# A three-part kernel on one core: 32-bit low words in the weight narrowing, attention buffers laid out by when the last batch frees them, and a new written order

## The chip, the cores and the metric

One core of a Trainium2 chip runs the whole program. The metric is the device time of one execution in microseconds (us). TensorE (PE) does the matmuls, VectorE (DVE), ScalarE (ACT) and GpSimd (POOL) the rest, and SyncE's queue (SP) issues every DMA.

## The reference, cut to what matters

```python
out_d  = sm_attn(mean4(q), mean4(k), mean4(v))        # attention over groups of four positions
out_up = np.repeat(out_d, 4, axis=2)
attn   = softmax(where(abs(i - j) < 4, scale * q @ k.T, -1e9))   # a band of seven positions
x = out_up + attn @ v                                  # batch 4, heads 8, 576 positions, 64 wide
x = x.transpose(0, 2, 1, 3).reshape(2304, 512)
x = (x @ w_a) * (x @ w_b) @ w_out                      # first pair: 512 -> 1536 -> 512
h = x @ w_in
y = (max(h, 0) + alpha * min(h, 0)) @ w_out2           # second pair: 512 -> 2048 -> 512
```

q, k and v come as 32-bit floats, the four weight matrices as 64-bit floats, alpha as 32-bit.

## The kernel before, in words

The 2304 positions are x's columns. The attention runs in 24 tiles of 96 positions, six to a batch (`turn`, `bound`, `soft`, `p_turn`, `av_t`), and once per batch over the means of four (`g_top`, `g_minus`, `g_exp`, `g_out`, `od_turn` for batches 0 and 1; `g_soft`, `g_turn`, `g_av` for 2 and 3). `x_add` adds both parts for one tile and writes x as a pair of 16-bit halves, scaled. `s1(j, f)` is the first matmul pair for block j (288 positions, eight blocks) and 128 hidden columns f (twelve), `s2(j, d)` its output, `x2_out(j)` stores it to DRAM. `s3` and `s4` are the second pair, in six blocks of 384. Every product is three 16-bit matmuls (high by high, high by low, low by high).

**Weights.** A matrix arrives as 64-bit floats in a staging buffer. `narrow(raw, dst)` makes 32-bit floats of them with integer operations: ACT scales the low 32-bit word down by 2^-29 (`activation`, an unsigned 32-bit input), DVE cleans the 16-bit piece beside it, DVE shifts the high word into `dst`, and POOL adds the two. For `w_a`, `w_b` (chunks `wab0` to `wab5`, each of two halves of 1024 elements per partition) and `w_in` (`wi0` to `wi3`, the same size), ACT then squares for a bound, a small PE and DVE chain makes a scale, and ACT and DVE split into two 16-bit halves. `w_out` (`wow`) and the second `w_out` (`wo2w`) go by 128 rows, 512 elements per partition.

**Buffers.** `zone` is one buffer of 19968 floats per partition. While the attention runs it holds the attention's tiles, cut off by `carve` one after another. Later it holds `wi` (floats 0 to 9215), `wo2` (9216 to 17919; its upper part also serves as the four staging buffers `raws2` of `w_in`, 2048 floats each from 9728 on) and `xr2`, two staging buffers of 1024 floats each from 17920 on. So a load of `w_in` may only start when the attention's tiles under its staging buffer are dead. Before the change the order in `zone` is: `gz` (0; the second set of first-pair results, used for blocks 1 and 3), `raw_z`, `qk_z` (8064), `e_z`, `xt_z` (12800, the attention's result that `x_add` reads), `odt`, `gq_z`, `gk_z`, `vd`, `od_z`.

**Order.** Nothing runs in the order of the calls. `Plan` records every operation with a planned cost, finds which regions overlap, and does one list schedule: on each engine the ready operation with the highest `prio` goes next, where `prio` is the planned length of what still follows plus a bias, and an operation inherits the `prio` of what depends on it:

```python
o.prio = max([o.tail + o.bias] + [s.prio + self.lat(o, s) + d for s in o.succ])
```

The calls are sorted by a time (`on(t, ...)`) only to say who writes a shared buffer first. The bias of a call is its own plus the entry of `URGENT` for its name (t0@3 is tile 3 of batch 0, t@1 all tiles of batch 1, x@0 the `x_add` of batch 0). The chain of `s1` to `s4` on PE is fixed. The schedule is then issued as it stands, and each engine works its own list in that order, whatever the chip's real times are. Where PE has a planned gap up to plan time 200, `fill` puts matmuls on the identity matrix into it: 0.7 of the gap divided by 0.112 us each.

Of the kernel before, what the change touches and what calls it, by code (L numbers as in the profile page):

```python
# [12 lines left out]
U32 = mybir.dt.uint32  # L13
# [12 lines left out]
class Plan:  # L26
# [66 lines left out]
    def cost(self, eng, method, out, ins, kw):  # L93
        n = self.free(out)
        if eng == self.PE:
            if method == "transpose":
                n = self.free(out)
                w = 2 if ins[0].dtype == F32 else 1
            else:
                w = 4 if ins[0].dtype == F32 else 1  # L100
            return max(0.03, n * w * 0.000425)
        m = max([n] + [self.free(a) for a in ins])
        if eng == self.POOL:
            return 0.2 + m * (0.0026 if method == "tensor_tensor" else 0.0011)
        if eng == self.ACT:
            if ins and ins[0].dtype == U32:
                return 0.2 + 0.00243 * m
            return 0.2 + 0.0009 * m + (0.19 if kw.get("accum_out") is not None else 0)
        if out.dtype == I16:
            return 0.1 + 0.00144 * m  # L110
        if method in ("tensor_scalar", "tensor_copy", "memset", "tensor_scalar_mul"):
            return 0.12 + 0.0009 * m
        return 0.14 + 0.0011 * m
# [130 lines left out]
    def fill(self, t0, t1, chain, early, stat, mov, each):  # L244


        pe = [o for o in self.order if o.eng == self.PE]
        f = self.nc.tensor.matmul
        add = []
        for a, b in zip(pe, pe[1:]):  # L250
            n = int(0.7 * (b.start - a.end) / each)
            if n < 2 or not t0 <= a.end < t1:
                continue
            g = next(o for o in chain if o.start >= b.start)
            if g is chain[0]:
                out = early
            else:
                if not g.calls[0][2]["start"] or any(p.end > a.end - 0.5 for p in g.preds if p.eng in (self.DVE, self.ACT)
                                                     and p.name[:2] in ("s1", "s2")):
                    continue  # L260
                out = g.calls[0][1][0]
            o = self.new(self.PE)
            o.calls = [(f, (out[:, :mov.shape[1]], stat, mov), dict(start=True, stop=True))] * n
            o.start, o.end = a.end + 1e-6, b.start
            o.name, o.n = "fill", -1
            add.append(o)
        self.order = sorted(self.order + add, key=lambda o: o.start)
# [11 lines left out]
def kernel(  # L279
# [27 lines left out]
    def A(method, *a, **kw):  # L307
        P("scalar", method, *a, **kw)
# [7 lines left out]
    B, H, S, D = q.shape  # L316
# [146 lines left out]
    def narrow(raw, dst):  # L463


        w = raw.bitcast(I32).rearrange("p (n t) -> p n t", t=2)
        h = raw.bitcast(I16).rearrange("p (n t) -> p n t", t=4)
        A("activation", out=h[:, :, 0], in_=raw.bitcast(U32).rearrange("p (n t) -> p n t", t=2)[:, :, 0],
          func=ACTF.Copy, scale=2.0 ** -29)
        V("tensor_scalar", out=h[:, :, 1], in0=h[:, :, 3], scalar1=-0x4000, scalar2=None, op0=ALU.bitwise_and)  # L470
        d = dst.bitcast(I32)
        V("tensor_scalar", out=d, in0=w[:, :, 1], scalar1=3, scalar2=0x3FFFFFFF,
          op0=ALU.logical_shift_left, op1=ALU.bitwise_and)
        G("tensor_tensor", out=d, in0=d, in1=w[:, :, 0], op=ALU.add)
# [60 lines left out]
    pool_m = const.tile([WK, 3, 120], F32, name="pool_m")  # L535
    LR = 3 * H * D
    gf, xf = flat(gt).bitcast(F32), x2s.bitcast(F32)
    gz = carve(F1 * N1)
    gt2 = gz.bitcast(F16).rearrange("p (a f n) -> p a f n", a=2, f=F1)
    raw_z = [carve(LR)[:WK] for _ in range(3)]  # L540
    raw_h = [gf[:WK, :LR], gf[:WK, LR:2 * LR], xf[:WK, :LR], gz[:WK, :LR], gz[:WK, LR:2 * LR]]
    LQ = H2 * (TQ + WK)
    qk_z = [carve(LQ) for _ in range(4)]
    e_z = [carve(H * TQ)[:WK].rearrange("p (h n) -> p h n", h=H) for _ in range(2)]
    xw = KD * TQ
    xt_z = [t.rearrange("p (a n) -> p a n", a=KD) for t in
            [const.tile([128, xw], F32, name="xt0")] + [carve(xw) for _ in range(TPB - 1)]]
    odt = carve(KD * NP).rearrange("p (a n) -> p a n", a=KD)
    gq_z = [carve(H2 * NP).rearrange("p (a n) -> p a n", a=H2) for _ in range(2)]
    gk_z = [carve(H2 * NP).rearrange("p (a n) -> p a n", a=H2) for _ in range(2)]  # L550
    pt = [raw_z[g][:HALF, :H * NP].rearrange("p (i n) -> p i n", i=H) for g in range(2)]
    vd = [carve(H * (D + 1))[:HALF].rearrange("p (h d) -> p h d", h=H) for _ in range(2)]
    od_z = carve(2 * DM)[:HALF]
    od = od_z.rearrange("p (u d) -> p u d", u=2)
    vraw = od_z.rearrange("p (h r d) -> p h r d", h=H // 2, r=FAC)
    vst = [const.tile([128, TPB], F32, name=f"vst{i}") for i in range(2)]
# [656 lines left out]

    tl = max(xtime.values()) + 5.0
    on(tl, alphas, "alphas", 20.0)
    for i in range(4):
        on(tl, lambda i=i: wi_load(i), f"wil{i}", 20.0)
    for c in range(DF2 // CW // 2):
        on(tl + 1 + 10 * c, lambda c=c: wi_chunk(c), f"wi{c}", 20.0)
    t2 = tl + 42  # L1220
    for i in range(2):
        on(t2, lambda i=i: wo2_load(i), f"wo2l{i}", 20.0)
# [17 lines left out]
    def group(name):  # L1240
# [5 lines left out]
        if name[:3] in ("s1_", "s2_"):  # L1246
# [1 line left out]
        return kind if kind in ("wow", "wos", "wo2w", "wo2s") else name  # L1248


    URGENT = {"alphas": -35, "bs0": -60, "bs1": -115, "bs2": 15, "bs3": -25, "gexp0": -45, "gexp1": -90,
# [13 lines left out]

    cal.sort(key=lambda x: x[:2])
    for _, _, fn, P.name, bias, P.rel in cal:
# [37 lines left out]
```

## Time and profile before

| | |
|---|---|
| median of 3 runs | 1039.46 us (1034.23 to 1042.77) |
| profiled execution | 1042.84 us, span 1041.1 us |
| PE busy | 1004.1 us, 96% of the span, 7631 matmuls |
| DVE busy | 611.7 us, 59% |
| ACT busy | 512.1 us, 49% |
| POOL busy | 140.4 us, 13% |

The times of the trace are microseconds from the span's start; the chip's time of an execution holds a little outside the span as well. PE's busy time counts the matmuls of `fill` too, and a matmul that runs at the lower clock counts for twice as long, so it doesn't say how much of the work is needed. The granted clock stands as a share of 2.4 GHz: 1.00 is 2.4 GHz throughout, 0.50 would be 1.2 GHz throughout.

### The profile page before, as it was taken

The page shows a single profiled execution, that of the slowest core. Times are in us where ns is not written, and L with a number is a line of the kernel's source. Part 1 is how long each engine was busy: PE and PEld are TensorE (multiplying, and loading weights), DVE is VectorE, ACT ScalarE, POOL GpSimd, SP SyncE. Part 2 cuts the span into 40 slices and gives each one's busy share as a digit, 9 for nine tenths or more (in the row PEclk, how much of TensorE's full clock was granted, in tenths as well). Part 3 has the DMA queues.
Part 4 walks back from the last instruction along what each step waited for, and adds up shares of the span by engine and source line. Part 5 has one row for each costly group of instructions (what it writes and reads, how often), then busy time and mean ns, then how long its engine had stood idle before and what let it go on. Part 6 is the DMA issues. An engine that isn't in the chain of part 4 may idle for free.

```text
span 1041.1 us, 18632 instructions
## 1 busy us (share of the span) xinstructions
PE 1004.1 (96%) x7631; PEld 694.1 (67%) x7631; DVE 611.7 (59%) x1245; ACT 512.1 (49%) x967; POOL 140.4 (13%) x128
## 2 busy tenths in 40 slices
PE   8889799989999999999979999999999999999998
PEld 5677577768787787887756777654645555454553
DVE  5899998857656866567868777540514415042240
ACT  3677688544333444345666775451615426062350
POOL 2345742002200020000244120000000000000000
PEclk9889999989999999999989999999999999999999
DMA  9674551014310063111561421010010200000000
GB/s 161 227 210 145 148 142 34 1 26 85 70 48 1 23 108 91 25 65 42 163 220 41 128 82 47 2 31 31 1 51 11 64 21 21 30 12 11 21 1 31
DMA packets 95942, 69.50 MB, mean 67 GB/s; under 512 B 71152, under 2 KB 78704, under 8 KB 95856
## 3 DMA queue, kind: packets, MB, share of 16 engines
q1 hardware_dynamic: 95856, 68.31, 24.8%
q8 instruction: 60, 0.98, 0.4%
q14 instruction: 26, 0.21, 0.1%
HBM read 58.86 MB, written 9.44 MB: 66 GB/s over the span
## 4 chain that ended last, share of the span: by engine, by line
PE 84%; DVE 8%; SPq 2%; ACT 2%; issue 2%; DMA 1%; POOL 1%; POOLq 0%; DVEq 0%
PE m L272 74%; PE a L272 8%; SPq L272 2%; DVE zone L272 2%; DVE wo L272 2%; DVE wab L272 1%; DMA zone<-in_v_dram 1%; PE r L272 1%; ACT zone L272 1%; ACT wo L272 1%; POOL zone L272 1%; DVE xt L272 0%; DVE ws L272 0%; DVE gm L272 0%; DVE gn L272 0%
## 5 line engine op out<-in xcount | busy, mean ns | idle before, releaser
L272 PEld LDWEIGHTS <-wab 128*128 128x128 f16 x3168 | 307.8, 98 | 164.0 <-issue 6.4
L272 PE MATMUL m<-xt,wab 128*128 128x288 f16 x2304 | 297.4, 287 | 4.9 <-DVE tm L272 2.3
L272 DVE SCALAR_TENSOR_TENSOR gt<-tm,nal,tm 128x384 f32<-128x384 f32 x96 | 59.3, 618 | 220.8 <-ACT tm L272 220.8
L272 PE MATMUL m<-xt,zone 128*128 128x384 f16 x1152 | 188.5, 326 | 0.0
L272 PE MATMUL m<-zone,wab 128*128 128x512 f16 x864 | 187.5, 379 | 0.0
L272 PEld LDWEIGHTS <-zone 128*128 128x128 f16 x1152 | 112.6, 98 | 74.8
L272 ACT ACTIVATE tm<-m 128x384 f32<-128x384 f32 (+1 forms) x224 | 97.5, 477 | 105.7 <-PE m L272 102.9
L272 PEld LDWEIGHTS <-wo 128*128 128x128 f16 x1152 | 112.2, 99 | 38.7 <-issue 9.2
L272 POOL TENSOR_TENSOR zone<-zone 72x256 f32<-72x256 f32 (+2 forms) x60 | 77.6, 1301 | 390.3 <-DVE zone L272 178.5
L272 PE MATMUL m<-gt,wo 128*128 128x288 f16 x864 | 114.1, 291 | 7.6 <-DVE gt L272 5.5
L272 ACT ACTIVATE zone<-zone 96x832 f32<-96x832 f32 (+5 forms) x73 | 81.7, 1150 | 31.5 <-DVE zone L272 24.9
L272 ACT ACTIVATE gt<-m,uf 128x512 f32<-128x512 f32 x18 | 12.4, 687 | 164.8 <-PE m L272 164.8
L272 PE MATMUL a<-zone 64*96 64x104 f32 (+4 forms) x1104 | 76.7, 272 | 4.9 <-DVE zone L272 3.8
L272 PEld LDWEIGHTS a<-zone 64*96 64x96 f32 (+4 forms) x1104 | 62.1, 155 | 22.9 <-issue 15.2
L272 ACT COPY zone<-a 104x384 f32<-104x384 f32 (+4 forms) x124 | 53.8, 476 | 40.7 <-PE a L272 40.3
L272 ACT COPY tm<-m 128x288 f32<-128x288 f32 x96 | 38.8, 404 | 67.5 <-PE m L272 64.1
L272 DVE SCALAR_TENSOR_TENSOR tm<-m,tm 128x288 f32<-128x288 f32 x96 | 43.5, 454 | 38.3 <-PE m L272 33.0
L272 DVE SCALAR_TENSOR_TENSOR wab<-gt,kap,wab 128x384 f16<-128x384 f32 x96 | 58.8, 614 | 8.3 <-ACT wab L272 8.3
L272 ACT ACTIVATE wab<-gt,kap 128x384 f16<-128x384 f32 x96 | 59.0, 616 | 1.5 <-DVE gt L272 1.5
L272 PE MATMUL m<-idf 128*128 128x256 bf16 x375 | 53.2, 293 | 0.0
L272 PE MATMUL a<-idf,zone 96*104 96x96 f32 (+4 forms) x392 | 42.8, 249 | 5.3 <-DVE zone L272 4.2
L272 ACT ACTIVATE gt<-tm 128x288 f16<-128x288 f32 x72 | 31.7, 443 | 32.0 <-DVE tm L272 31.7
(172 smaller groups left out, 948.0 us busy)
## 6 DMA issues: line engine op xcount, KB each, us to landing
zone<-in_moe_w_out_dram SPq DMA_DIRECT2D x16, 512.0 KB
zone<-in_moe_w_in_dram SPq DMA_DIRECT2D x8, 1024.0 KB
wo<-in_moe_w_a_dram SPq DMA_DIRECT2D x6, 1024.0 KB
wo<-in_moe_w_b_dram SPq DMA_DIRECT2D x6, 1024.0 KB
x_d<-x2s SPq DMA_DIRECT2D x8, 576.0 KB
out_dram<-gt SPq DMA_DIRECT2D x18, 256.0 KB
zone<-in_k_dram SPq DMA_DIRECT2D x21, 208.0 KB
zone<-in_v_dram SPq DMA_DIRECT2D x21, 208.0 KB
```

The lines of the kernel that those rows point to most:

```text
L272: f(*args, **kw)
```

## The change

1. In `narrow`, ACT writes its scaled low word as a 32-bit integer (`w[:, :, 0]`) and no longer as a 16-bit one (`h[:, :, 0]`); the DVE operation on the 16-bit piece beside it then writes over half of that word and has to follow it. The planned cost of that ACT operation falls from 0.2 + 0.00243 to 0.2 + 0.00095 us per element.
2. `zone` is cut in another order: `e_z`, two of the four `qk_z`, `raw_z`, the `gq`/`gk` of odd batches, one `vd`, `od_z`, the `gq`/`gk` of even batches, the other two `qk_z`, `gz`, `xt_z`, `odt`, the other `vd`. Under the first three staging buffers of `w_in` (9728 to 15871) then lie `od_z`, the even batches' `gq` and `gk`, two `qk_z` and `gz`; under the fourth (15872 to 17919) `gz` and `xt_z`; under `xr2` `xt_z`, `odt` and `vd`.
3. The loads `wil0` to `wil2` and the chunk `wi0` are called at the end of the last batch's tiles, ahead of its `x_add`, and not after it. `wil3` and the other chunks stay.
4. `fill` takes 0.3 of a gap where it begins before plan time 30, and 0.7 later as before.
5. `URGENT` has other values nearly everywhere; some of them stand below.

```diff
             if ins and ins[0].dtype == U32:
-                return 0.2 + 0.00243 * m
+                return 0.2 + 0.00095 * m
...
-            n = int(0.7 * (b.start - a.end) / each)
+            n = int((0.3 if a.end < 30.0 else 0.7) * (b.start - a.end) / each)
...
-        A("activation", out=h[:, :, 0], in_=raw.bitcast(U32).rearrange("p (n t) -> p n t", t=2)[:, :, 0],
+        A("activation", out=w[:, :, 0], in_=raw.bitcast(U32).rearrange("p (n t) -> p n t", t=2)[:, :, 0],
           func=ACTF.Copy, scale=2.0 ** -29)
...
+    e_z = [carve(H * TQ)[:WK].rearrange("p (h n) -> p h n", h=H) for _ in range(2)]
+    qk_z = [carve(LQ) for _ in range(2)]
+    raw_z = [carve(LR)[:WK] for _ in range(3)]
+    gq1, gk1 = heads(NP), heads(NP)
+    vd = [carve(H * (D + 1))[:HALF].rearrange("p (h d) -> p h d", h=H)]
+    od_z = carve(2 * DM)[:HALF]
+    gq_z, gk_z = [heads(NP), gq1], [heads(NP), gk1]
+    qk_z += [carve(LQ) for _ in range(2)]
     gz = carve(F1 * N1)
...
+    te = first[B - 1] + pace[B - 1] * TPB
     for i in range(4):
-        on(tl, lambda i=i: wi_load(i), f"wil{i}", 20.0)
+        on(tl if i == 3 else te, lambda i=i: wi_load(i), f"wil{i}", 20.0)
     for c in range(DF2 // CW // 2):
-        on(tl + 1 + 10 * c, lambda c=c: wi_chunk(c), f"wi{c}", 20.0)
+        on(tl + 1 + 10 * c if c else te + 1, lambda c=c: wi_chunk(c), f"wi{c}", 20.0)
```

Of `URGENT`, before and after: t0@3 -35, -85; t0@4 -45, 70; t0@5 15, 115; x@0 -5, 25; wab0 -25, 50; wab1 15, 30; wab2 65, -85; wab3 -145, 80; wab4 45, -35; wab5 -135, -55; wow 65, none; wi0 40, 5; wi1 -40, 10; wi2 45, 50; wi3 -100, 50.

## Rows read from the trace of the kernel before

**Rows 1.** Windows by stage: engines' busy us (instructions), granted clock, DMA share, GB/s.

```profile
0.00:30.00 30.00, 25.16 (x194) 17.96 (x195) 19.03 (x41) 10.71 (x21) 7.76 (x44) 1.00 1.04 192
30.00:121.00 91.00, 76.62 (x709) 60.94 (x707) 84.31 (x139) 62.96 (x74) 46.44 (x21) 0.87 0.62 185
200.00:240.00 40.00, 37.01 (x345) 28.91 (x343) 25.23 (x66) 17.66 (x35) 0.00 (x0) 0.91 0.15 29
240.00:520.00 280.00, 279.88 (x2595) 223.19 (x2593) 191.70 (x424) 121.58 (x259) 28.89 (x28) 1.00 0.27 65
520.00:562.00 42.00, 31.86 (x233) 23.62 (x232) 32.92 (x38) 28.04 (x34) 20.87 (x10) 0.89 0.52 164
562.00:663.00 101.00, 100.38 (x807) 79.11 (x806) 71.27 (x170) 63.89 (x122) 14.13 (x11) 0.99 0.22 67
663.00:1041.00 378.00, 374.30 (x2020) 197.35 (x2018) 115.74 (x209) 147.34 (x311) 0.00 (x0) 1.00 0.07 23
```

**Rows 2.** Groups of PE, 30 to 121: fill's matmuls, and the first pair's.

```profile
L272 PE MATMUL m<-idf 128*128 128x256 bf16 x285 | 39.4, 294 | 0.0
L272 PE MATMUL m<-xt,wab 128*128 128x288 f16 x50 | 6.6, 286 | 2.2 <-DVE xt L272 1.9 <-ACT xt L272 0.2
```

**Rows 3.** Timeline of PE, 62 to 140, the first pair's start: us, duration, count.

```profile
86.91 6.05 PE L272 MATMUL m<-xt,wab 128*128 128x288 f16 x48
...
120.96 5.92 PE L272 MATMUL m<-xt,wab 128*128 128x288 f16 x47 [1.93 <-DVE xt L272]
```

**Rows 4.** Timeline of PE: the first matmuls of the second pair.

```profile
662.94 17.23 PE L272 MATMUL m<-xt,zone 128*128 128x384 f16 x105
```

**Rows 5.** Timeline of PE, 520 to 562: matmuls, and idle before them with its releaser.

```profile
526.72 0.28 PE L272 MATMUL m<-gt,wo 128*128 128x288 f16 x1 [2.10 <-ACT gt L272]
531.89 0.88 PE L272 MATMUL m<-gt,wo 128*128 128x288 f16 x3 [4.88 <-DVE gt L272]
533.35 6.10 PE L272 MATMUL m<-gt,wo 128*128 128x288 f16 x38 [0.59 <-DVE gt L272]
539.40 7.51 PE L272 MATMUL m<-gt,wo 128*128 128x288 f16 x60
...
558.88 9.18 PE L272 MATMUL m<-xt,wab 128*128 128x288 f16 x60 [2.33 <-DVE tm L272]
```

**Rows 6.** Timeline of ACT around that stall.

```profile
518.99 7.12 ACT L272 ACTIVATE zone<-zone 128x1024 int16<-128x1024 uint32 x4
525.82 0.53 ACT L272 COPY tm<-m 128x288 f32<-128x288 f32 x1
```

**Rows 7.** Timeline of DVE around that stall.

```profile
523.85 6.30 DVE L272 TENSOR_SCALAR zone<-zone 128x1024 int16<-128x1024 int16 x4 [0.73 <-ACT zone L272]
529.95 0.47 DVE L272 SCALAR_TENSOR_TENSOR tm<-m,tm 128x288 f32<-128x288 f32 x1
```

**Rows 8.** Timeline of SP: loads of `w_in` before and after the stall's begin.

```profile
459.41 15.97 SPq L272 DMA_DIRECT2D zone<-in_moe_w_in_dram  x2
...
504.82 6.55 SPq L272 DMA_DIRECT2D zone<-in_moe_w_in_dram  x2
```

**Rows 9.** Groups of ACT, whole span, shapes apart: busy us, mean ns.

```profile
L272 ACT ACTIVATE wo<-wo 128x1024 int16<-128x1024 uint32 x12 | 30.1, 2510 | 0.0
L272 ACT ACTIVATE zone<-zone 128x512 int16<-128x512 uint32 x16 | 21.3, 1363 | 1.9 <-DMA zone<-in_moe_w_out_dram 1.9
...
L272 ACT ACTIVATE wab<-wab 128x1024 bf16<-128x1024 f32 x12 | 12.6, 1056 | 5.3 <-DVE wab L272 3.3 <-POOL wab L272 2.0
...
L272 ACT ACTIVATE zone<-zone 128x512 bf16<-128x512 f32 x16 | 10.2, 638 | 4.6 <-POOL zone L272 4.4
```

**Rows 10.** Groups of DVE, 30 to 121: `narrow`'s two operations.

```profile
L272 DVE TENSOR_SCALAR wo<-wo 128x1024 int16<-128x1024 int16 x12 | 16.9, 1412 | 0.1
L272 DVE TENSOR_SCALAR wab<-wo 128x1024 int32<-128x1024 int32 x12 | 9.9, 827 | 0.0
```

**Rows 11.** The chain that ended last, its shares of the span by line.

```profile
by line: PE m L272 74.4%; PE a L272 8.4%; SPq L272 2.4%; DVE zone L272 1.8%; DVE wo L272 1.7%; issue 1.6%; DVE wab L272 1.2%; DMA zone<-in_v_dram 1.1%; PE r L272 0.9%; ACT zone L272 0.8%; ACT wo L272 0.7%; POOL zone L272 0.6%; DVE xt L272 0
```

More of the change, by code (lines that the diff above doesn't have):

```diff
@@ L537, with heads @@
     gf, xf = flat(gt).bitcast(F32), x2s.bitcast(F32)
+    xw = KD * TQ
+    def heads(n):
+        return carve(H2 * n).rearrange("p (a n) -> p a n", a=H2)
+    LQ = H2 * (TQ + WK)
+    e_z = [carve(H * TQ)[:WK].rearrange("p (h n) -> p h n", h=H) for _ in range(2)]
[6 more added lines that the diff above has]
+    qk_z += [carve(LQ) for _ in range(2)]
     gz = carve(F1 * N1)
     gt2 = gz.bitcast(F16).rearrange("p (a f n) -> p a f n", a=2, f=F1)
-    raw_z = [carve(LR)[:WK] for _ in range(3)]
     raw_h = [gf[:WK, :LR], gf[:WK, LR:2 * LR], xf[:WK, :LR], gz[:WK, :LR], gz[:WK, LR:2 * LR]]
[L542 to L545, printed above, removed]
     xt_z = [t.rearrange("p (a n) -> p a n", a=KD) for t in
@@ L548 @@
     odt = carve(KD * NP).rearrange("p (a n) -> p a n", a=KD)
-    gq_z = [carve(H2 * NP).rearrange("p (a n) -> p a n", a=H2) for _ in range(2)]
-    gk_z = [carve(H2 * NP).rearrange("p (a n) -> p a n", a=H2) for _ in range(2)]
+    vd.append(carve(H * (D + 1))[:HALF].rearrange("p (h d) -> p h d", h=H))
     pt = [raw_z[g][:HALF, :H * NP].rearrange("p (i n) -> p i n", i=H) for g in range(2)]
-    vd = [carve(H * (D + 1))[:HALF].rearrange("p (h d) -> p h d", h=H) for _ in range(2)]
-    od_z = carve(2 * DM)[:HALF]
     od = od_z.rearrange("p (u d) -> p u d", u=2)
@@ L1248, in group @@
         return kind if kind in ("wow", "wos", "wo2w", "wo2s") else name
-    URGENT = {"alphas": -35, "bs0": -60, "bs1": -115, "bs2": 15, "bs3": -25, "gexp0": -45, "gexp1": -90,
[13 rows of a table removed]
+    URGENT = {"alphas": 5, "bs0": 90, "bs1": -15, "bs2": -25, "bs3": 15, "gexp0": -80, "gexp1": -35,
[12 rows of a table added]
     cal.sort(key=lambda x: x[:2])
```

25 rows, old and new, of the table URGENT are left out of this document.

## The prediction

> **What bounds the kernel now.** I read the windows by stage first [rows 1]; the reader is to see three kinds of stage in them. From 663 on PE is busy all but 3.7 of 378 us at clock 1.00, and the second pair's first matmul stands at 662.94 [rows 4]; none of the edits changes that pair's matmuls, so the end comes 378 us after this start, and whatever is won has to be won ahead of it. From 240 to 520 PE is busy 279.88 of 280 us at full clock: nothing to win there either, only to lose. What is left is the head, 0 to 121, and two holes.
>
> In the head PE looks busy (76.62 of 91 us from 30 to 121), but 39.4 us of that are fill's 285 matmuls on the identity, and only 50 matmuls of the first pair run [rows 2]. Their start is 86.91, then the chain on PE stands until 120.96, where it waits for DVE to write x [rows 3]. DVE is busy 84.31 of those 91 us: in the head the bound is DVE's list and its order. The first hole is 200 to 240: 40 - 37.01 = 3.0 us idle, and a clock of 0.91 costs (1 - 0.91) x 37.01 = 3.3 us more, 6.3 in all. The second is 520 to 562. PE waits 2.10 + 4.88 + 0.59 + 2.33 = 9.9 us there for ACT and DVE, and two groups run slowly after the waits: 38 matmuls take 6.10 us where 60 take 7.51 (0.125 each, so 4.76), and 60 take 9.18, together 1.3 + 1.7 = 3.0 us [rows 5]. That is 12.9 us; the window's own numbers, 10.1 idle and 0.11 x 31.86 = 3.5 for the clock, give 13.6 [rows 1].
>
> The timelines of ACT and DVE say what PE waited for in the second hole. ACT works on four narrowings without a pause, 7.12 us from 518.99, and only then reads out the first pair's PSUM bank (525.82) [rows 6]; DVE does four of its 16-bit narrowing operations, 6.30 us from 523.85, and then its half of that eviction at 529.95 [rows 7]. The evictions were late only because the list had put the weights of the second pair in front of them. The weights themselves were not urgent: the stall is over at 562, the second pair starts at 663.
>
> **ACT's narrowing, written as 32-bit words.** It removes no instruction. One takes 2510 ns for 1024 elements and 1363 for 512. How long it takes with a 32-bit result no row shows. From below it is bounded by ACT operations of the same length that read 32-bit floats and write without gaps, 1056 and 638 ns; from above by today's 2510 and 1363 [rows 9], since nothing is added to it, and on DVE the 32-bit operation (827 ns) is cheaper than the 16-bit one on as many elements (1412) [rows 10]. By that last pair I take a value near the low end, 1.2 and 0.7 us. There are 20 of the long ones (12 + 8) and 28 of the short ones (12 + 16): 20 x 1.3 + 28 x 0.66 = 44.5 us of ACT's time. Most of that is beside other work. On the chain that ended last ACT's writes to `wo`, nearly all of them these narrowings in the head, hold 0.7% of 1041.1 = 7.3 us [rows 11]; of those 1.3/2.5 can go, 3.8 at most. I take 3.0, because DVE, next in line, has little idle time to start earlier in. The DVE operation on the 16-bit piece now has to follow ACT's. In the trace it already did: in the stall it begins after a wait for ACT [rows 7]. So no new wait is priced; if it were one, all of DVE's list would stand behind it for up to 2.5 us each time, and shorter ACT operations make that smaller, not larger.
>
> The Trainium skill's page "ScalarE: Activation LUTs", section "What ACT_TABLE_LOAD costs", gives 186 ns and 0.833 ns per element, the same for fp32 and bf16. By it today's operation would be estimated at 1.04 us where the row has 2.51, so trace and page differ. Read strictly, a rate that doesn't depend on the type says that another type of result changes nothing: then these 3.0 us are missing and the sum is 17, not 20.
>
> **The head's new order.** All twelve halves of `w_a` and `w_b` are narrowed on DVE ahead of 121, 16.9 + 9.9 = 26.8 us, 2.24 each [rows 10], while the chain on PE up to its second start needs the first two chunks' four halves. By the biases before, wab2 (65) and wab4 (45) could go ahead of tile 5 (15). Now tile 5 has 115 and tile 4 70, wab2 -85, wab4 -35, wab5 -55; only wab3 (80) rises, and with three staging buffers its halves need the first half of wab2 out of the way, so that one inherits the rank. Five halves then can go behind tile 5's x: 5 x 2.24 = 11.2 us. That is the upper end; the lower is 0, if tile 5's own chain through four engines is what takes so long. I take half, 5.5. What is late next is the rest of DVE's list: it has to be done while the chain runs, and there is room (191.70 busy of 280 us from 240 on).
>
> **Fewer fill matmuls before plan time 30.** PE is busy 25.16 of the first 30 us at clock 1.00 [rows 1]. Removing fill shortens what queues on PE there by little, since the tiles' data are still coming (DMA share 1.04). What it could cost is the clock: at the 0.87 of the next stage those 25.16 us would be 28.9, so at most +3.8. I take 0 and keep 3.8 for the range. The Trainium skill's page "TensorE: Matmul & The Clock Gate", section "Part 1: The HAM clock gate", says that the slow clock is the default and activity releases it; it speaks against this edit. The rows bear it out in part, as the clock falls in 30 to 121, with its waits, and in spite of 285 fills. By it the sum is 16.
>
> **The new layout and the early loads.** No instruction is added; the DMAs are the same 8 loads of `w_in` and 16 of the second `w_out`. Before, two loads of `w_in` go out at 459.41 and behind it, and the next two at 504.82 [rows 8], after x's last tiles. With three staging buffers under tiles that die earlier, the first three loads need only the last tiles' `qk_z` and `gz`, and chunk wi0 the last `e_z`; so wi0 can be narrowed, bounded and split before 505, which also frees two buffers for loads 4 and 5. Room for it is there: from 240 to 520 ACT is busy 121.58 and DVE 191.70 of 280 us [rows 1]. A chunk is two halves; its DVE work in `narrow` is 2 x 2.24 = 4.5 us and its ACT work 2 x 1.2. The weights aren't awaited by the second pair, so all that this earns is a shorter queue in front of the evictions of 520 to 562: the four narrowings of ACT fall from 7.1 to some 3.5 us if nothing is moved, and lose a third or more of their number if the chunk is. I take 9.5 of the 12.9 us; ends 0 and 13.6. On SP the early loads stand in line ahead of the stores of x2 and the late loads; one issue is short and PE waits for neither. `xr2` now lies under `xt_z` and `odt`, so the loads of the second `w_out` can't start before x is done; they are used only after 663, and this stays hidden as long as they are done by then. For the first hole, where batch 1's ends meet the order, I take 2 of 6.3 us, since a new order hits or misses it by chance.
>
> **Sum.** 3.0 + 5.5 + 0 + 9.5 + 2 = 20 us. The profiled execution took 1042.84 us (span 1041.1 and 1.7 around it), 3.4 above the median of the runs shown; 1042.8 - 20 = 1022.8, and by the median 1039.5 - 20 = 1019.5. I forecast 1020.
>
> **The rivals.**
> *The early start is larger.* The head gives its bounds, 3.8 + 11.2, and both holes close, 13 + 6: 34 us, 1005. For it speaks that DVE is full in the head and that weights are what fills it; against it that a new order can open a hole as well as close one. 0.12.
> *The stall stays in its place.* The fourth load, the later chunks and now the second `w_out` too still wait for x's last tiles, and their narrowings meet the same evictions. Then only the head gives, 8.5 us: 1031. For it speaks that the stall came right after x's last tiles and that the lists are fixed by planned times. 0.22.
> *The new ACT operation is as slow as the old one,* while the plan reckons with 0.2 + 0.00095 per element: the change doesn't do what it says. Up to 1.3 us of lateness per long narrowing then stand in ACT's list, the 3.0 are missing and half of the second hole stays: 20 - 3 - 6 = 11 won, 1028. 0.09.
> *Slower: the bunch moves into the full stretch.* If the list puts wi0's narrowings ahead of evictions between 459 and 505, and the load lands later than planned, ACT and DVE hold those evictions as they did in [rows 6, 7], and PE, which has no spare time there, loses a stall of 12.9 us for each such bunch. With the old stall kept and two new ones, less 8.5 from the head and 2 from the first hole, it comes to +15, 1055. It decides from the point at which a load lands behind its planned time by more than PE's lead over the evictions. For it speaks that this happened once; against it that ACT and DVE are half and a third idle there, and that the two bunches would have to be as long as the old one. 0.10.
>
> **How the numbers follow.** The forecast has 0.47 and reaches from 1010 to 1030. The range is to leave out the slower rival (0.10) and the far half of the largest gain: 1004 to 1040. A change of less than 1% (10.4 us) is about what a measurement of this kernel can't tell from none. Faster by more than that, below 1029: 0.43 of the forecast, 0.12, 0.05 of the stall that stays, 0.05 of the slow ACT operation, 0.65. Slower by more, above 1050: 0.08. Between: 0.27.
>
> **What would show it.** Right: ACT's narrowing groups near 1.2 and 0.7 us; the first pair's second start at some 112 and not 120.96; a load of `w_in` before 459 and wi0's last split before 520; PE idle under 4 us in the stretch that follows x's last tiles; the second pair's first matmul near 643, with 378 us behind it as now. Wrong: the ACT groups unchanged; the second start at 121 or later, or a clock under 1.00 in the first 30 us; a wait of PE for ACT or DVE of several us anywhere between 240 and the second pair.

## The result, and the profile after

The changed kernel takes 1026.07 us (median of 4 runs, 1025.41 to 1027.12), the kernel before 1040.64 beside it (4 runs, 1034.23 to 1042.77): a ratio of 0.9871, 95% interval 0.9826 to 0.9917, so 1.3% faster. Its profiled execution took 1027.12 us, span 1025.4, 15.7 less than before's 1041.1.

Windows of the changed kernel, by the stages of [rows 1], with the same columns:

```profile
0.00:30.00 30.00, 23.00 (x185) 15.93 (x186) 20.46 (x43) 11.98 (x22) 7.76 (x44) 1.00 1.03 229
30.00:121.00 91.00, 74.01 (x677) 58.90 (x676) 88.39 (x142) 44.66 (x73) 49.82 (x24) 0.88 0.59 175
200.00:240.00 40.00, 38.34 (x356) 29.91 (x354) 25.68 (x68) 18.46 (x38) 0.00 (x0) 0.91 0.23 40
240.00:520.00 280.00, 278.11 (x2576) 221.48 (x2575) 195.54 (x432) 120.56 (x260) 32.29 (x29) 1.00 0.26 65
520.00:562.00 42.00, 42.00 (x342) 33.18 (x341) 38.76 (x63) 24.15 (x53) 22.85 (x12) 1.00 0.54 174
```

Timeline of PE of the changed kernel, lines that answer to [rows 3], [rows 5] and [rows 4], with two groups between them:

```profile
81.50 7.59 PE L272 MATMUL m<-xt,wab 128*128 128x288 f16 x47 [2.40 <-DVE xt L272]
...
118.03 8.36 PE L272 MATMUL m<-xt,wab 128*128 128x288 f16 x47 [2.51 <-DVE xt L272]
126.89 1.64 PE L272 MATMUL m<-xt,wab 128*128 128x288 f16 x12
...
246.41 7.51 PE L272 MATMUL m<-xt,wab 128*128 128x288 f16 x60
...
520.53 17.80 PE L272 MATMUL m<-gt,wo 128*128 128x288 f16 x144
...
647.20 13.00 PE L272 MATMUL m<-xt,zone 128*128 128x384 f16 x79
```

The kernel before has the same groups at these times:

```profile
127.37 1.64 PE L272 MATMUL m<-xt,wab 128*128 128x288 f16 x12
...
249.16 7.51 PE L272 MATMUL m<-xt,wab 128*128 128x288 f16 x60
...
520.78 3.84 PE L272 MATMUL m<-gt,wo 128*128 128x288 f16 x30
```

The second pair starts at 647.20 instead of 662.94, 15.7 us earlier, and is followed by 378.2 us as before (1025.4 - 647.2): all of the gain lies ahead of it. PE works through the same chain of matmuls in the same order in both kernels. So where the gain arises can be read from when one and the same matmul starts in the two traces:

| the same matmul of the chain | before | after | lead |
|---|---|---|---|
| second start of the first pair | 120.96 | 118.03 | 2.93 |
| the next group, 47 matmuls later | 127.37 | 126.89 | 0.48 |
| first of a group behind the first hole | 249.16 | 246.41 | 2.75 |
| first of the `s2` behind 520 | 520.78 | 520.53 | 0.25 |
| start of the second pair | 662.94 | 647.20 | 15.74 |

Nearly all of the gain, 15.5 us, arises behind 520. In 520 to 562 PE is busy 42.00 of 42 us at clock 1.00, and 144 matmuls of `s2` follow each other where three waits stood. Windows of the whole stretch up to the second pair of the kernel before, that kernel first, then the changed one:

```profile
520.00:663.00 143.00, 132.23 (x1038) 102.73 (x1037) 104.19 (x207) 91.94 (x156) 35.01 (x20) 0.96 0.31 96
520.00:663.00 143.00, 143.00 (x1130) 110.25 (x1129) 105.68 (x209) 82.30 (x172) 34.55 (x20) 1.00 0.28 91
```

Before, 10.8 us of it are idle and the clock costs another 0.04 x 132.23, some 5.3; after, nothing is lost.

The 2.93 us of the second start don't last. The 47 matmuls behind it take 8.36 us (granted clock 0.70 from 118.03 to 126.40), where before they take 5.92 (1.00 from 120.96 to 126.90). The three kernels further down in which they also stand behind a wait of 2.51 us (16-bit operation, `fill` at 0.7, old layout) take 8.67, 8.47 and 8.44 for them. Between 249 and 520 the lead falls again: in 240 to 520 PE now idles 1.9 us, where it idled 0.1. The table compares one execution of each kernel, and the executions of the kernel before lie up to 8.5 us apart, so its steps of 2 or 3 us are readings of these two traces and no more.

ACT's narrowing groups of the changed kernel, whole span, shapes apart, against [rows 9]: 2510 ns have become 1154, 1363 have become 673.

```profile
L272 ACT ACTIVATE wo<-wo 128x1024 int32<-128x1024 uint32 x12 | 13.9, 1154 | 0.3 <-DMA wo<-in_moe_w_b_dram 0.3
...
L272 ACT ACTIVATE zone<-zone 128x512 int32<-128x512 uint32 x16 | 10.7, 673 | 0.0
```

Timelines of the changed kernel for what filled the hole before: SP's loads of `w_in`, against [rows 8], and ACT's narrowings of that matrix, against [rows 6]. Taken one by one, the four narrowings in that row are two halves of `w_in` (1024 elements) and two pieces of the second `w_out` (512), which lie in `zone` too.

```profile
430.82 12.47 SPq L272 DMA_DIRECT2D zone<-in_moe_w_in_dram  x2
459.16 18.57 SPq L272 DMA_DIRECT2D zone<-in_moe_w_in_dram  x3
517.11 0.38 SPq L272 DMA_DIRECT2D zone<-in_moe_w_in_dram  x1
526.57 4.73 SPq L272 DMA_DIRECT2D zone<-in_moe_w_in_dram  x2
```

```profile
438.28 1.14 ACT L272 ACTIVATE zone<-zone 128x1024 int32<-128x1024 uint32 x1
456.36 1.13 ACT L272 ACTIVATE zone<-zone 128x1024 int32<-128x1024 uint32 x1
...
482.84 1.14 ACT L272 ACTIVATE zone<-zone 128x1024 int32<-128x1024 uint32 x1
486.50 1.17 ACT L272 ACTIVATE zone<-zone 128x1024 int32<-128x1024 uint32 x1
```

Five of the eight loads are out before 480, and five of the eight narrowings are done by 488, each alone between other work. Before, two were done by 486, and the next two stood without a pause at 518.99, with the two of the second `w_out`. The head is another matter. A piece of the chain that ended last, of the changed kernel (start, us, what):

```profile
108.71 6.75 DVE zone L272 x3
```

This piece by DVE's timeline, with an earlier operation of the same kind ahead of it, and POOL's timeline beside it:

```profile
81.38 0.54 DVE L272 TENSOR_TENSOR zone<-zone 128x384 f32<-128x384 f32 x1
...
105.84 2.87 DVE L272 TENSOR_SCALAR wab<-wo 128x1024 int32<-128x1024 int32 x1
108.63 5.91 DVE L272 TENSOR_TENSOR zone<-zone 128x384 f32<-128x384 f32 x1
```

```profile
101.79 6.37 POOL L272 TENSOR_TENSOR wab<-wab,wo 128x1024 int32<-128x1024 int32 x1 [2.37 <-issue]
108.12 1.17 POOL L272 TENSOR_TENSOR zone<-zone 72x256 f32<-72x256 f32 x1
109.26 2.53 POOL L272 TENSOR_TENSOR wo<-wo,x2s 128x512 int32<-128x512 int32 x2
111.75 2.38 POOL L272 TENSOR_TENSOR wab<-wab,wo 128x1024 int32<-128x1024 int32 x1
```

An operation of DVE that takes 0.54 us at 81.38 takes 5.91 at 108.63. POOL works without a gap from 108.12 to 114.13, on one operation of the attention and then on three integer additions; DVE's operation begins within that time and ends at 114.54, just behind it. DVE's write of x, for which PE waits until 118.03, stands behind it in the list. For most of the 5.91 us DVE can't have been working; a busy row can be a waiting row. The whole trace of the changed kernel bears this out. DVE's eviction `gt<-gt,tm` of 288 columns, which reads both inputs from SBUF, takes 0.45 us in the mean and at most 0.48 in the 54 cases in which POOL does nothing meanwhile, and 0.89 in the mean and up to 2.65 in the 18 others. `tm<-m,tm`, which reads one input from PSUM, takes 0.45 and 0.46. POOL seems to wait too: its addition at 101.79 takes 6.37 us, the one at 111.75 takes 2.38.

The kernel before has such rows in its second hole as well. Taken one by one, the four operations of DVE at 523.85 in [rows 7] are three of the 16-bit kind and a 32-bit one, of 2.71, 0.77, 2.58 and 0.72 us. The two long ones take 1.31 and 0.44 elsewhere, and stand beside these additions:

```profile
522.95 2.44 POOL L272 TENSOR_TENSOR zone<-zone 128x1024 int32<-128x1024 int32 x1 [5.76 <-DVE zone L272]
526.64 2.58 POOL L272 TENSOR_TENSOR zone<-zone 128x1024 int32<-128x1024 int32 x1 [1.25 <-DVE zone L272]
```

So some 3.5 of DVE's 6.30 us there are waiting, not narrowing.

### The profile page after: what moved, and what is told of

It is laid out like the page before. It is cut to its first block, busy times and chain, and to the rows that moved or that the text cites. A ratio compares the mean times of both kernels' runs of the same rounds, so it can differ in the third digit from the quotient of the medians.

```text
span 1025.4 us, 18493 instructions
## 1 busy us (share of the span) xinstructions
PE 993.8 (97%) x7565; PEld 686.7 (67%) x7565; DVE 610.9 (60%) x1245; ACT 470.6 (46%) x967; POOL 139.8 (14%) x128
## 4 chain that ended last, share of the span: by engine, by line
PE 88%; DVE 9%; issue 1%; DMA 0%; ACT 0%; POOL 0%; SPq 0%; DVEq 0%; POOLq 0%; ACTq 0%
PE m L272 78%; PE a L272 9%; DVE zone L272 2%; DVE wo L272 2%; DVE wab L272 1%; PE r L272 1%; DVE xt L272 1%; DVE gt L272 1%; DVE x2s L272 0%; DVE nm L272 0%; DVE gm L272 0%; DMA zone<-in_v_dram 0%; DVE vst L272 0%; DVE nz L272 0%; DVE gn L272 0%
## 5 line engine op out<-in xcount | busy, mean ns | idle before, releaser
L272 PE MATMUL m<-gt,wo 128*128 128x288 f16 x864 | 111.8, 288 | 0.9 <-DVE x2s L272 0.9
L272 ACT ACTIVATE zone<-zone 96x832 f32<-96x832 f32 (+5 forms) x73 | 61.5, 847 | 38.9 <-DVE zone L272 28.2
L272 POOL TENSOR_TENSOR wab<-wab,wo 128x1024 int32<-128x1024 int32 x12 | 37.7, 3148 | 58.2 <-DVE wo L272 31.0
```

The source lines that it names most:

```text
L272: f(*args, **kw)
```

## The experiments

The theory: the gain is the closed hole, and it comes from spreading the narrowings of `w_in`; the head gave little because DVE stands still beside POOL's additions. The rivals: the gain comes from the shorter ACT operation, from the order alone, or from fill. Each expectation names its own two sides. Ratios are against the kernel before on the same chip, whose medians were 1039.77 (7 runs), 1040.03 (19) and 1040.90 (10). "Of after" says that a kernel is the changed one with this edit, "of before" that it is the other one.

### The ACT operation and fill

**The 16-bit operation back, every list as in after** (the plan still reckons with the shorter one):

```diff
+        P.ops[-1].calls = [(nc.scalar.activation, (), dict(out=h[:, :, 0], in_=raw.bitcast(U32)...[:, :, 0],
+                                                           func=ACTF.Copy, scale=2.0 ** -29))]
```

> The changed kernel with its list of work unchanged on every engine, but ACT's low words written as 16-bit pieces again (2.51 and 1.36 us in place of 1.15 and 0.67). Theory A, early loads and order closed the hole after x's last tiles: the stretch of 42 us after 520 stays nearly free of waits (under 3 us idle on PE), the head's second start of the first pair moves from 118.0 by 1 to 3 us, and the time is 1028 to 1031, 2 to 5 above the changed kernel. Theory B, the shorter ACT operation closed it: PE idles there again for 6 us or more and the time is 1034 or above.

1028.77 us (1026.59 to 1031.03), ratio 0.9888 (0.9858 to 0.9919). By the medians the shorter operation is worth 2.7 us with the order fixed, by the ratios 1.8, near the 3.0 of the sum. But the four runs lie at 1026.6 and at 1030.9, two and two, and the interval covers after's 0.9871: the size is not settled. In its profile the second start is 119.89 and the hole opens by 1.7 us (windows):

```profile
520.00:562.00 42.00, 40.26 (x325) 31.54 (x324) 37.14 (x57) 29.79 (x48) 20.50 (x11) 1.00 0.52 164
```

So ACT's duration alone does not explain a hole of 12.9 us. The plan's shorter cost and the lists made with it stay in this kernel; what the lists would be with the old cost, it doesn't show.

**fill at 0.7 everywhere:**

```diff
-            n = int((0.3 if a.end < 30.0 else 0.7) * (b.start - a.end) / each)
+            n = int(0.7 * (b.start - a.end) / each)
```

> The changed kernel with fill at 0.7 of a gap from the start; every other list is the same. Theory A, fewer fill matmuls are worth next to nothing: within 1.5 us of the changed kernel's 1026. Theory B, the removed fill lets the tiles' matmuls go earlier: 1028 to 1031. Theory C, the removed fill costs clock: 1022 to 1024 with fill back, and a higher clock between 30 and 121 than 0.88.

1026.71 us (1025.28 to 1027.53), 0.9874 (0.9854 to 0.9895): no difference, with a second start at 117.82 (118.03 in after). The granted clock of 30 to 121 was 0.94 instead of 0.88, and bought nothing, because PE waits there anyway.

### The hole

**The narrowing of `w_in` shortened to 8 of 1024 columns, every list as in before.** It leaves out the low words and signs of nearly all of `w_in`.

```diff
+        if cut:   # and the same for DVE's 16-bit operation and POOL's addition
+            P.ops[-1].calls = [(nc.scalar.activation, (), dict(out=h[:, :8, 0], in_=...[:, :8, 0],
+                                                               func=ACTF.Copy, scale=2.0 ** -29))]
...
-        narrow(raw, slot(t, i))
+        narrow(raw, slot(t, i), t is wi)
```

> The kernel before with its list unchanged, but the narrowing of w_in runs on 8 of 1024 columns on ACT, on GpSimd and in DVE's 16-bit operation (8 halves; most of w_in's low words and signs are left out). Theory A, these operations standing in the lists ahead of the evictions make the hole of 520 to 562: PE idles under 3 us there, not 10.1, the second pair starts some 12 us earlier than 662.9, time 1026 to 1030. Theory B, PE waits for something else there (x's last tiles, a DMA): the hole stays above 7 us idle and the time within 4 us of the kernel before.

1028.01 us (1023.29 to 1028.91), 0.9879 (0.9850 to 0.9908). PE is busy 41.16 of 42 us where it was 31.86, and the second pair starts at 647.98. Without a change of layout or order, the time of these operations alone closes the hole: together they were its cause. ACT's, DVE's and POOL's operations are shortened at once here, so how much each had of it, and how much of DVE's share was standing beside POOL, isn't shown.

```profile
520.00:562.00 42.00, 41.16 (x332) 32.24 (x330) 26.65 (x62) 22.50 (x49) 11.67 (x11) 1.00 0.48 166
```

**Of after, with the layout and the calls of before** (`carve` in the old sequence, `wil0` to `wil2` and `wi0` at `tl`):

```diff
-        on(tl if i == 3 else te, lambda i=i: wi_load(i), f"wil{i}", 20.0)
+        on(tl, lambda i=i: wi_load(i), f"wil{i}", 20.0)
...
-        on(tl + 1 + 10 * c if c else te + 1, lambda c=c: wi_chunk(c), f"wi{c}", 20.0)
+        on(tl + 1 + 10 * c, lambda c=c: wi_chunk(c), f"wi{c}", 20.0)
```

> The changed kernel with the zone cut as before and the loads of w_in and wi0 called after x's last tiles as before; 32-bit low words, urgencies and fill stay changed, and the lists are sorted anew. Theory A, the layout with the early loads closed the hole after x's last tiles: PE idles 5 us or more in the 50 us from there, the second pair starts at 655 or later, time 1032 to 1040. Theory B, the shorter ACT operations and the new urgencies do it alone: under 3 us idle there, time 1024 to 1029.

1038.14 us (10 runs, 1033.82 to 1039.60), 0.9971 (0.9953 to 0.9988). By the medians 12 of the 14.6 us are gone, by the ratios 10 of 13, and PE waits in this stretch again:

```profile
520.00:562.00 42.00, 34.15 (x258) 26.07 (x256) 40.10 (x46) 20.81 (x39) 23.76 (x12) 0.94 0.51 165
```

The waits are not the same ones. 1.08 and 2.27 us are for evictions (`gt`, `x2s`), 0.75 and 3.75 for DVE in the small chain that makes a scale (`us_i`, `tr`).

**Of before, with the new layout and the early calls alone** (the same lines, the other way):

> The kernel before with the new zone and the early calls of the loads and of wi0 only; 16-bit low words, their old cost, the old urgencies and fill. Theory A, the layout closes the hole by itself: idle under 4 us in the 42 us after x's last tiles, time 1026 to 1031. Theory B, it needs urgencies that fit it: the hole is 7 us or more, or another opens between 240 and 520, time 1036 to 1048.

1040.86 us (10 runs, 1038.74 to 1041.70), 0.9998 (0.9986 to 1.0011): nothing. And yet the edit did what it says. Timeline of ACT, narrowings of `w_in` in this kernel:

```profile
440.47 2.49 ACT L272 ACTIVATE zone<-zone 128x1024 int16<-128x1024 uint32 x1
...
477.47 2.50 ACT L272 ACTIVATE zone<-zone 128x1024 int16<-128x1024 uint32 x1
490.16 2.51 ACT L272 ACTIVATE zone<-zone 128x1024 int16<-128x1024 uint32 x1
499.43 2.49 ACT L272 ACTIVATE zone<-zone 128x1024 int16<-128x1024 uint32 x1
```

Five are done by 502 and the bunch of four is gone. PE waits all the same, and DVE's timeline says for what:

```profile
528.15 19.40 PE L272 MATMUL m<-gt,wo 128*128 128x288 f16 x143 [6.21 <-DVE tm L272]
```

```profile
523.05 1.50 DVE L272 TENSOR_TENSOR zone<-zone 128x384 f32<-128x384 f32 x3
524.45 3.28 DVE L272 SCALAR_TENSOR_TENSOR xt<-zone,sx,xt 128x384 f16<-128x384 f32 x2
527.65 0.81 DVE L272 SCALAR_TENSOR_TENSOR tm<-m,tm 128x288 f32<-128x288 f32 x2
```

Now it is x's own additions and writes of the last tiles that the list has put ahead of the eviction (`tm` at 527.65). One bunch in the list has taken the place of another; the first of the two writes at 524.45 takes 2.75 us, where 0.61 is usual. The stretch of 42 us is a little better than before (35.27 us busy for 31.86), but from 562 to 663 PE now waits 4.0 us (97.00 busy of 101), where before it waited 0.6.

**Of after, with the old `URGENT`:**

```diff
-    URGENT = {...}   # the values of after
+    URGENT = {...}   # the values of before
```

> The changed kernel with the urgencies of before; layout, early calls, 32-bit low words and fill stay. Theory A, the layout and the shorter ACT operation together close the hole, whatever the urgencies: 1026 to 1031. Theory B, the layout pays only in an order that uses it: the hole after x's last tiles stays at 6 us or more and the time is 1034 to 1044.

1032.99 us (1031.65 to 1034.10), 0.9924 (0.9910 to 0.9938), between the two sides. Half of the gain goes without the new order; the windows have PE busy 36.01 of 40 us in 200 to 240, 275.23 of 280 and 39.81 of 42 behind it.

**Of before, with the 32-bit operation and its planned cost alone:**

```diff
-                return 0.2 + 0.00243 * m
+                return 0.2 + 0.00095 * m
...
-        A("activation", out=h[:, :, 0], ...
+        A("activation", out=w[:, :, 0], ...
```

> The kernel before with the 32-bit low words and their cost in the plan alone; lists sorted anew. Theory A, by the sum of the prediction the shorter operation is worth 3 us and half of the hole at most: 1032 to 1038. Theory B, a new order with the old layout and urgencies wins nothing or loses: 1038 to 1046. In both ACT's operation takes 1.15 and 0.67 us.

1044.84 us (1042.24 to 1045.15), 1.0030 (1.0016 to 1.0044): slightly slower, though ACT saves what it saves in after (45.82 us busy from 30 to 121, where [rows 1] has 62.96). The hole has other waits (timeline of PE):

```profile
535.84 8.70 PE L272 MATMUL m<-gt,wo 128*128 128x288 f16 x48 [5.29 <-DVE x2s L272]
...
565.28 4.71 PE L272 MATMUL m<-xt,wab 128*128 128x288 f16 x24 [4.05 <-DVE tm L272]
```

**Of before, with the new `URGENT` alone** (the diff above, the other way):

> The kernel before with the new urgencies alone. Theory A, they carry the head's and half of the rest's gain by themselves: 1028 to 1036. Theory B, they fit only the plan for which they were chosen (with the layout and the new cost): no faster than before, 1038 or more.

1045.60 us (1043.67 to 1045.98), 1.0042 (1.0028 to 1.0056): slower too.

So by the ratios the operation, the order and the layout alone give +3, +4 and 0 us, two of the three -3 (operation and order), -8 (operation and layout) and -12 (layout and order, with the plan's new cost), all of them -13. The gain belongs to none of the three alone, and most of it needs the layout with the early loads and an order that uses them: with those two and the 16-bit operation -12 of the -13 are there. Whether that order could be found without the new cost in the plan stays open; no kernel here has the layout and the new `URGENT` with the old cost.

### The head

**Of after, POOL's additions for `w_a` and `w_b` on 8 of 1024 columns.** It leaves out the low words and signs of nearly all of these weights.

```diff
+        if cut:
+            P.ops[-1].calls = [(nc.gpsimd.tensor_tensor, (), dict(out=d[:, :8], in0=d[:, :8], in1=w[:, :8, 0], op=ALU.add))]
```

> The changed kernel with its list unchanged, but GpSimd's add in the narrowing of w_a and w_b runs on 8 of 1024 columns (12 operations; sign and low bits of the first weights are left out). Theory A, the head waits for DVE's own work and for the last tile's chain through four engines: the second start stays within 2 us of 118.0, time 1024 to 1026. Theory B, DVE's operations stand still while GpSimd works, and that holds up x in the head (a DVE operation of 0.54 us took 5.91 at 108.6): the long DVE operations go, the second start falls by 6 to 15 us, to 103 to 112, and the time to 1011 to 1020.

1003.17 us (1001.61 to 1005.97), 0.9652 (0.9627 to 0.9677), 22.9 us less than after and more than either side expected. The second start is 96.60, and in the same 91 us PE does 875 matmuls where after does 677:

```profile
30.00:121.00 91.00, 86.40 (x875) 70.60 (x874) 87.19 (x182) 60.23 (x108) 36.06 (x31) 0.98 0.72 204
```

POOL is at 55% of the stage in after (49.82 of 91 us), half idle, and holds the head all the same: either as the additions are slow themselves, in a chain from DVE over POOL to ACT, or as they hold DVE.

**Of after, each of these twelve additions in four pieces of 256 columns**, with nothing left out:

```diff
+        if cut:
+            m = d.shape[-1] // 4
+            P.ops[-1].calls = [(nc.gpsimd.tensor_tensor, (), dict(out=d[:, i * m:(i + 1) * m], in0=d[:, i * m:(i + 1) * m],
+                                                                  in1=w[:, i * m:(i + 1) * m, 0], op=ALU.add))
+                               for i in range(4)]
```

> The changed kernel with its lists unchanged, but each of GpSimd's 12 adds in the narrowing of w_a and w_b is issued as four of 256 columns; nothing is left out. Theory A, DVE stands still for as long as one GpSimd instruction runs, so a shorter instruction frees it sooner: the DVE operation of 5.91 us at 108.6 falls below 3, the second start of the first pair comes 3 to 8 us before 118.0, time 1018 to 1023. Theory B, what the run with 8 columns won was the shorter wait for the add itself: the four pieces take as long or longer together, so the second start stays or comes later, time 1025 to 1030.

1018.53 us (6 runs, 1016.15 to 1024.46), 0.9767 (0.9748 to 0.9785): less than after by 7.5 us (by the medians; by the ratios 10.8), and better than both kernels. On POOL the additions are slower, not faster. Groups of POOL, after first, then this kernel:

```profile
L272 POOL TENSOR_TENSOR wab<-wab,wo 128x1024 int32<-128x1024 int32 x12 | 37.7, 3148 | 58.2 <-DVE wo L272 31.0 <-DVE nz L272 10.3 <-issue 7.3
```

```profile
L272 POOL TENSOR_TENSOR wab<-wab,wo 128x256 int32<-128x256 int32 x48 | 52.9, 1136 | 47.7 <-DVE wo L272 25.0 <-DVE ux L272 7.5 <-issue 7.1
```

A half takes 4 x 1.14 = 4.5 us instead of 3.15. A piece that nothing disturbs takes 0.72, four of them 2.9, so a good part of the 4.5 is waiting too, now on POOL's side. It is DVE that gains: it is busy 80.42 us from 30 to 121, where after has 88.39. The two operations shown above for after, here on DVE's timeline:

```profile
112.08 1.19 DVE L272 TENSOR_SCALAR wab<-wo 128x1024 int32<-128x1024 int32 x1
113.19 1.09 DVE L272 TENSOR_TENSOR zone<-zone 128x384 f32<-128x384 f32 x1
```

2.87 and 5.91 us have become 1.19 and 1.09. That the time falls though the additions last longer speaks against the addition's own duration as the cause and for DVE's standing still. It holds for the direction; how the 22.9 us of the cut additions divide between the two stays open. And the theory's other sign failed: in the profiled execution, the longest of the six, the second start is 119.24, not 3 to 8 us earlier than 118.03. Its second pair starts at 644.20, 3.0 ahead of after, and most of that arises in 200 to 240, where its granted clock is 1.00 and after's is 0.91. So this profile doesn't show the head's gain, and where the other executions win the rest isn't seen.

**Of after, all of POOL's additions of the narrowing in pieces of 256:**

```diff
+        P.ops[-1].calls = [(nc.gpsimd.tensor_tensor, (), dict(out=d[:, i:i + 256], in0=d[:, i:i + 256],
+                                                              in1=w[:, i:i + 256, 0], op=ALU.add))
+                           for i in range(0, d.shape[-1], 256)]
```

> The changed kernel with unchanged lists and every add of GpSimd in the narrowing (all four weight matrices) issued in pieces of 256 columns; nothing is left out. Theory A, DVE's standstill is paid per GpSimd instruction wherever DVE is full: a little better than with w_a and w_b alone, 1014 to 1018. Theory B, outside w_a and w_b DVE has idle time enough: within 2 us of that run's 1018.5.

1023.21 us (1019.78 to 1026.23), 0.9824 (0.9800 to 0.9848): better than after, worse than the twelve alone, as neither side expected. In its profile the head does gain: the second start is 114.75, the 47 matmuls behind it take 5.92 us, and the next group starts at 121.17, 5.7 us before after's 126.89. PE loses 2.9 us in 240 to 520 (busy 277.12; 278.50 with the twelve alone). Whether the longer additions there cost this, and where the rest of the 4.7 us between the two medians goes, stays open.

**Of after, the low word put in by DVE with an or, no addition on POOL for `w_a`, `w_b`** (ACT's scale a little smaller, so that the bits don't meet; the lowest bits round otherwise; the plan orders the lists anew):

```diff
-        G("tensor_tensor", out=d, in0=d, in1=w[:, :, 0], op=ALU.add)
+        if cut:
+            V("tensor_tensor", out=d, in0=d, in1=w[:, :, 0], op=ALU.bitwise_or)
+        else:
+            G("tensor_tensor", out=d, in0=d, in1=w[:, :, 0], op=ALU.add)
```

> The changed kernel, but the low word of w_a and w_b (scaled to 0 to 7) is put in by a bitwise or on DVE, not by an add on GpSimd, with DVE's cost in the plan, so the lists are sorted anew; the lowest bits of the weights are rounded a little otherwise. Theory A, the standstill is the larger cost: 12 more DVE operations of some 1.2 us, 14 us, against about 18 us of standstill and 2.4 us of latency each: second start 4 to 10 us before 118.0, time 1016 to 1023. Theory B, DVE's own work is the bound: the second start comes 5 to 14 us later than 118.0, time 1030 to 1038.

1021.49 us (1019.02 to 1025.02), 0.9815 (0.9784 to 0.9845). The head is nearly as good as with the cut additions (866 matmuls in 30 to 121 for 875, first start 75.50 for 67.89), though DVE has more to do, 89.74 us busy. It is lost again in the full stretch, where another order brings 12.7 us of waits for DVE's evictions:

```profile
30.00:121.00 91.00, 85.57 (x866) 69.35 (x865) 89.74 (x166) 54.57 (x93) 26.02 (x15) 1.00 0.64 178
...
240.00:520.00 280.00, 267.31 (x2410) 211.04 (x2408) 187.26 (x408) 118.27 (x250) 29.62 (x23) 0.97 0.25 67
```

## Why the prediction was right, and where its steps were off

It said 1020; it was 1026.07, within the forecast's own 1010 to 1030, and the hole that it put most of the gain into did close. Its terms fared less well than their sum. Those that lie ahead of 520 (3.0, 5.5 and 2, together 10.5 us) came to a lead of 0.3 us at 520, and the one behind it (9.5) came to 15.5. That the two errors, 10 too much and 6 too little, nearly cancel is luck.

**The ACT operation.** Taken as 1.2 and 0.7 us, measured 1.15 and 0.67. Its 3.0 us stand beside 2.7 by the medians and 1.8 by the ratios, measured with the order fixed, a difference with a wide interval. The rival that the type of the result changes nothing fell. The Trainium skill's page "ScalarE: Activation LUTs", section "What ACT_TABLE_LOAD costs", gives one rate for fp32 and bf16, by which an estimate for 1024 elements is 1.04 us; the 32-bit row (1154 ns) comes near it, the 16-bit one (2510) doesn't.

**The head's order, 5.5 us: this step failed.** The prediction let two or three halves of `w_a` and `w_b` go behind tile 5's x. They didn't: in after, all twelve of DVE's 16-bit operations still begin ahead of that x, the last at 104.74, the write of x at 117.38. Groups of DVE, 30 to 121, against [rows 10]:

```profile
L272 DVE TENSOR_SCALAR wo<-wo 128x1024 int16<-128x1024 int16 x12 | 19.0, 1586 | 0.0
L272 DVE TENSOR_SCALAR wab<-wo 128x1024 int32<-128x1024 int32 x11 | 11.5, 1055 | 0.0
```

The first start came 5.4 us earlier (86.91 to 81.50), the second only 2.9, and of these 0.5 were left 47 matmuls later, since those ran at a lower granted clock: with the ACT operation's share, 0.5 for the 8.5 expected. What an earlier start costs in clock had no term. The same operations also take longer, 1586 and 1055 ns for 1412 and 827; in the kernel with pieces of 256 they have 1377 and 769. The view that DVE is busy 84.31 of 91 us was read as work. Part of it was waiting beside POOL, which the prediction did not price, and the kernel before has such rows too: there an operation on 384 elements took 2.66 us at 115.39, where 0.54 at 73.77.

**The second hole, 9.5 of 12.9: right in place and cause, too small.** All of it closed, and 15.5 us were won between 520 and the second pair, more than the 13.6 that were set as the upper end: up to 663 the stretch had lost 10.8 us idle and 5.3 to the clock. The kernel of before with the short narrowings shows that these made the hole, the one of after with the old layout that the layout is needed to spread them. But moving the chunk was half of the story: the layout alone moved five narrowings and won nothing. The condition that x's writes and the evictions are put in another order as well wasn't in the prediction. Two readings were off. Of the four narrowings of ACT in that stall only two were of `w_in`, and of DVE's 6.30 us some 3.5 were waiting beside POOL.

**The full stretch.** The slower rival didn't come true: narrowings between 438 and 488 cost no stall there. PE idled 1.8 us more in 240 to 520, in waits of 0.45 to 0.91 us, and the lead fell by 2.5, which had no term. **The first hole** gave 1.2 by the windows (6.3 lost before; 1.7 idle and 0.09 x 38.34 = 3.4 for the clock after), for 2 taken; with the stretch ahead of it the lead grew by 2.3. **Fill** was taken at 0 and is 0. The clock of the first 30 us stayed 1.00.

**The signs named beforehand.** A load of `w_in` before 459: 430.82. wi0's last split before 520: missed, DVE's ended at 522.8. PE idle under 4 us behind x's last tiles: 0. The second pair near 643: 647.20, with 378 us behind it. The second start near 112: missed, 118.03. All in all the sum of 20 became 15.7 in the profile: 8.0 too much in the head, 0.3 too little from there through the first hole, 2.5 unforeseen in the full stretch, and 6.0 too little behind 520.

## What to carry to other kernels

Where each engine works a fixed list, ask of every moved step what the list puts into the place that comes free; an edit that does just what it says can win nothing until the order around it changes as well, so try the parts together and alone. A long busy time on DVE beside POOL isn't yet work: compare the same operation's shortest duration with its longest, and try POOL's operations in shorter pieces before moving anything. A shorter operation off the critical path is worth what the path has of it, here some 2 or 3 us of the 44.5 at which the prediction put ACT's saving. And judge an earlier start by a matmul well behind it: 2.9 us at the second start were 0.5 after 47 matmuls.

## What was not expected of the hardware

DVE stands still beside POOL: 0.54 us became 5.91 while POOL ran four operations in a row, and at 105.84 an operation that otherwise has some 0.7 took 2.87. Only DVE operations that meet one of POOL's are long: in the changed kernel's trace the 1044 that meet none lie within 0.12 us of the shortest one of their shape, and the 201 others are together some 61 us above it. The Trainium skill's page "SBUF — State Buffer", section "Who interferes with whom", says that a DVE instruction with two inputs in SBUF contends with a GpSimd instruction that reads SBUF, that the lock on the ports they share is exclusive, and that issue order decides who blocks. The 5.91 us row agrees, with four of POOL's instructions in its wait; so do the evictions with both inputs in SBUF, 0.89 us beside POOL for 0.45 alone. That pieces of 256 columns let DVE through at a cost to POOL (4.5 us a half for 3.15) and win 7.5 us by the medians is what the runs add to it.

A 16-bit result, written eight bytes apart, costs ACT more than twice the 32-bit one at the same distance: 2510 against 1154 ns for 1024 elements, 1363 against 673 for 512.
